# Sums over tokens of a tile in two halves instead of one operation, with the instruction order searched anew

## Chip, cores, metric

One core of one Trainium2 chip. The metric is device time in microseconds (us) of one execution. The kernel before takes 383.95 us (median of 3 runs, 383.66 to 384.04). "Span" is the time from the first to the last instruction in the trace of one execution; it is some 1.8 us shorter than the measured time.

## The reference

Two layers, each of a linear attention (A) and a gated MLP (B), on x of 2048 tokens x 512, with 32 heads of 16 columns and 1376 columns in the MLP. What the change touches are `kv` and `z`, the sums over all tokens:

```python
phi_k = concat([softmax(pk), softmax(-pk)], -1)      # per head; pk = k @ w_phi
kv  = einsum("bhsf,bhsd->bhfd", phi_k, v)            # sum over tokens s
z   = einsum("bhsf->bhf", phi_k)
num = einsum("bhqf,bhfd->bhqd", phi_q, kv)           # attention needs the complete sums
den = einsum("bhqf,bhf->bhq", phi_q, z)[..., None] + 1e-6
x = x + ((num / den) merged) @ wo
...
gate = gate * (gate > 0);  x = x + (gate * up) @ W_down
```

## The kernel before

It works on 16 tiles of 128 tokens. The program describes some 2100 operations with their dependences, buffers and a due time each (table `DUE`) and, for those that two engines can do, a place (`PLACE`: copies out of PSUM on ScalarE or VectorE, halves of phi on GpSimd or VectorE). A planner turns this into one order for every engine; both tables come from a search. TensorE's order therefore isn't in the code but in the tables.

The keys of one tile (cut):

```python
k  = op("PE", ..., name="K")                 # 4 products: pk, with w_phi folded into the weight
e  = [op("ACT", ..., Exp, scale=+1/-1)]      # ek, two halves
v  = op("PE", ..., name="V"); v = evac(...)  # vext: v and a column of ones
a  = op("DVE", SUM16, tensor_reduce(ek))     # sk: sums per head; then Ln and Exp on ScalarE: 1/sum
...
parts = []
for k, e in enumerate(PHI[phi_eng]):         # two halves of 32 rows of heads each
    parts.append(op(e, cost, due, f, [a], ..., name="phi", alt=...))  # phiK = ek * sk, VectorE or GpSimd
a = parts

def kvz():
    for g in range(NG):                      # NG = 8
        b, k = g // 2, g % 2
        nc.tensor.matmul(self.bufs[k].t[:, b * GV:(b + 1) * GV],
                         lhsT=ph.t[:, g, :, :].rearrange("p s e -> p (s e)"), rhs=vx.t[:, g, 0:GV],
                         start=(self.n == 0 and b == 0), stop=(self.n == T - 1), skip_group_check=True)
    self.n += 1
first = not self.sums
z = op("PE", SUMS, due_z, kvz, a + [v] + (self.before if first else self.sums[:1]),
       self.bufs if first else [], [ph, vx] + ([] if first else self.bufs), name="kvz")
self.sums.append(z)
```

After 16 tiles VectorE turns the two PSUM buffers of sums into `R`, and the attention products (`erq`, Eq times R) can start. TensorE then works on projections, gate, up and down products; layer 1's keys lie among them.

Filler products: up to the first sum over tokens, the program puts products on zeros where the plan foresees an idle TensorE:

```python
for o in order:
    if o.eng == "PE":
        filling = filling and o.name != "kvz"
        if filling and free is not None:
            idle(max(0, int((o.start - free - 150) / FILL)))     # products of zeros, 216 ns each
        free = o.start + o.spent
    o.emit()
```

The softmax here doesn't subtract the row's maximum and nothing guards it: scores larger than these inputs give would overflow.

## Time and profile before

| | before |
|---|---|
| time, median | 383.95 us |
| span | 382.0 us |
| TensorE busy, work by count | 371.5 us, 368.8 us |
| VectorE, ScalarE, GpSimd busy | 311.1, 215.0, 41.9 us |
| halves of phi | 38 on GpSimd, 26 on VectorE |

The prediction shows how TensorE bounds the kernel. Two more rows of the kernel before belong to the argument: the makers of phi, in the groups by form (count, then busy us and mean ns of one, then idle time before them).

```profile
L879 POOL TENSOR_TENSOR phiK<-ek,sk 128x512 bf16<-128x512 bf16 x38 | 41.2, 1102 | 192.3 <-ACT sk L870 164.1 <-DVE hT L1076 15.8 <-PE b L849 3.9
L879 DVE TENSOR_TENSOR phiK<-ek,sk 128x512 bf16<-128x512 bf16 x26 | 17.6, 703 | 0.1
```

A half of phi costs VectorE 0.70 us and GpSimd 1.10 us on average. And the view of the tile phiK lists who waited for it (us, times):

```profile
  DVE R L924: 2.0, 2
  POOL phiK L879: 1.9, 1
```

TensorE is not in the list: no sum over tokens was late for its phi.

### The profile page before, as it was taken

To read this page: it belongs to the slowest core of one execution; us is meant where nothing else is said; L and a number is where in the kernel's file an instruction comes from. 1 tells how busy PE (TensorE), PEld (TensorE's weight loads), DVE (VectorE), ACT (ScalarE), POOL (GpSimd) and SP (SyncE) were. 2 spreads that over 40 slices of the span, in tenths; PEclk is the share of its full clock that TensorE was granted. 3 is DMA by queue.
4 is the path that set the end of the run, shared out by engine and by line. 5 is a ranking of instruction groups with operands and counts; after the bars stand their busy time and mean duration, and the time that the engine had idled before them with its cause. 6 is when DMAs were issued, how large, how long until landed. Compare 5 with 4: busy or idle time off the path is not lost.

```text
span 382.0 us, 7622 instructions
## 1 busy us (share of the span) xinstructions
PE 371.5 (97%) x2787; PEld 224.4 (59%) x2832; DVE 311.1 (81%) x798; ACT 215.0 (56%) x554; POOL 41.9 (11%) x44
## 2 busy tenths in 40 slices
PE   7999998999989999999999999999999999999996
PEld 4545456967545445554656654696855544467575
DVE  7999999999999989983694677999998976763334
ACT  6999989636445316772455679984526412243040
POOL 0276710000200000230020124000000000000000
PEclk9999999999999999999999999999999999999999
DMA  8497720222221321211200100013322221020110
GB/s 232 122 205 219 188 89 2 52 58 62 57 56 41 44 54 40 45 23 27 45 6 15 22 8 1 2 36 70 77 44 70 57 56 56 14 62 16 41 50 29
DMA packets 60869, 22.83 MB, mean 60 GB/s; under 512 B 52672, under 2 KB 59808, under 8 KB 60832
## 3 DMA queue, kind: packets, MB, share of 16 engines
q1 hardware_dynamic: 60416, 21.95, 24.9%
q8 instruction: 22, 0.36, 0.4%
q10 hardware_dynamic: 416, 0.39, 0.4%
q14 instruction: 15, 0.12, 0.1%
HBM read 7.91 MB, written 2.10 MB: 26 GB/s over the span
## 4 chain that ended last, share of the span: by engine, by line
PE 77%; DVE 17%; DMA 2%; issue 2%; ACT 1%; DVEq 0%
PE b L1068 31%; PE b L1101 17%; PE b L855 5%; PE b L849 5%; PE b L992 5%; PE b L937 5%; PE q L955 3%; PE b L1044 2%; PE q L896 2%; DMA xnTA<-xn 2%; DVE pr L980 1%; DVE bstA L810 1%; DVE bstB L810 1%; DVE sk L860 1%; DVE N L753 1%
## 5 line engine op out<-in xcount | busy, mean ns | idle before, releaser
L1068 PE MATMUL b<-xnTB,wgu 128*128 128x128 bf16 (+2 forms) x1191 | 152.3, 279 | 0.5
L1068 PEld LDWEIGHTS <-wgu 128*128 128x128 bf16 x1200 | 97.7, 98 | 42.5
L1072 ACT ACTIVATE gu<-b 128x512 bf16<-128x512 f32 (+1 forms) x83 | 48.0, 584 | 63.7 <-PE b L1068 61.3
L1101 PE MATMUL b<-wd,hT 128*128 128x512 bf16 (+3 forms) x349 | 82.3, 372 | 0.7
L879 POOL TENSOR_TENSOR phiK<-ek,sk 128x512 bf16<-128x512 bf16 x38 | 41.2, 1102 | 192.3 <-ACT sk L870 164.1
L1101 PEld LDWEIGHTS <-hT 128*128 128x128 bf16 (+1 forms) x363 | 34.7, 98 | 33.9 <-DVE hT L1076 0.2
L1076 DVE TENSOR_TENSOR hT<-gu 128x512 bf16<-128x512 bf16 (+1 forms) x83 | 34.0, 414 | 15.4 <-ACT gu L752 14.2
L1108 DVE SCALAR_TENSOR_TENSOR X<-b,rsB,X 128x512 bf16<-128x512 f32 (+1 forms) x33 | 23.7, 729 | 23.8 <-PE b L1101 23.8
L752 ACT CAST gu<-b 128x512 bf16<-128x512 f32 (+1 forms) x50 | 28.4, 570 | 24.0 <-PE b L1068 20.4
L860 DVE TENSOR_REDUCE sk<-ek 128x64 f32<-128x1024 bf16 x32 | 38.6, 1210 | 2.7 <-ACT ek L852 2.3
L852 ACT ACTIVATE ek<-b 128x512 bf16<-128x512 f32 x64 | 36.0, 616 | 8.3 <-PE b L849 8.1
L941 ACT ACTIVATE Eq<-b 128x512 bf16<-128x512 f32 x64 | 37.3, 629 | 3.3 <-PE b L937 3.1
L752 ACT CAST N<-q 128x384 bf16<-128x384 f32 (+1 forms) x59 | 26.1, 464 | 12.4 <-PE q L955 6.7
L855 PE MATMUL b<-wv,xnTA 128*128 128x512 bf16 x123 | 31.9, 379 | 0.3
L937 PE MATMUL b<-xnTA,Wq 128*128 128x512 bf16 x125 | 31.9, 379 | 0.2
L849 PE MATMUL b<-Wk,xnTA 128*128 128x512 bf16 x123 | 31.6, 379 | 0.4 <-DVE xnTA L753 0.2
L992 PE MATMUL b<-wo,oT 128*128 128x512 bf16 x120 | 31.3, 379 | 0.4
L753 DVE CAST gu<-b 128x512 bf16<-128x512 f32 (+1 forms) x33 | 21.8, 665 | 11.1 <-PE b L1068 11.1
L955 PE MATMUL q<-R,Eq 128*128 128x144 bf16 x256 | 27.5, 226 | 1.8 <-DVE N L753 1.3
L955 PEld LDWEIGHTS <-Eq 128*128 128x128 bf16 x256 | 20.3, 98 | 13.1 <-issue 2.6
L980 DVE TENSOR_TENSOR pr<-N,w 128x1024 bf16<-128x1024 bf16 x32 | 21.8, 683 | 0.7
L810 DVE BATCH_NORM_STATS2 bstA<-X 128x6 f32<-128x512 bf16 x32 | 21.3, 682 | 1.2 <-DMA X<-in_A_x_dram 1.0
(75 smaller groups left out, 388.9 us busy)
## 6 DMA issues: line engine op xcount, KB each, us to landing
out_dram<-X SPq DMA_DIRECT2D x15, 128.0 KB, 1.7
X<-in_A_x_dram SPq DMA_DIRECT2D x6, 256.0 KB, 3.3
wgu<-in_B_W_gate_dram SPq DMA_DIRECT2D x4, 344.0 KB, 3.4
wgu<-in_B_W_up_dram SPq DMA_DIRECT2D x4, 344.0 KB, 3.5
wd<-in_B_W_down_dram SPq DMA_DIRECT2D x5, 256.0 KB, 3.5
wv<-in_A_wqkv_dram SPq DMA_DIRECT2D x2, 256.0 KB, 4.7
wo<-in_A_wo_dram SPq DMA_DIRECT2D x4, 128.0 KB, 3.1
oT<-o SPq DMA_TRANSPOSE x28, 2.3
```

Of the source, the lines that this page charges most:

```text
L752: both = {"ACT": ("ACT", act(cols), lambda: nc.scalar.copy(out=out_(), in_=in_()), False), "DVE": ("DVE", dve(cols), lambda: nc.vector.ten ...
L849: k = op("PE", mm(4, 512), due, lambda: [nc.tensor.matmul(kp.t[:], lhsT=xnTA[c][:, b, cols], rhs=Wk2[:, b, :], start=(b == 0), stop=(b == ...
L855: v = op("PE", mm(4, 512), due_v, lambda: [nc.tensor.matmul(vp.t[:], lhsT=xnTA[c][:, b, cols], rhs=wv[:, b, :], start=(b == 0), stop=(b == ...
L860: a = op("DVE", SUM16, due, lambda: nc.vector.tensor_reduce(out=sk.t[:, row, :], in_=ek.t[:].rearrange("p g s (h f) -> p (g s h) f", f=DH) ...
L879: e.tensor_tensor(out=ph.t[:].rearrange("p g s (h f) -> p (g s h) f", f=DH)[:, lo:lo + n], in0=ek.t[:].rearrange("p g s (h f) -> p (g s h) ...
L937: q = op("PE", mm(4, 512), due(c, b), lambda b=b, qp=qp: [nc.tensor.matmul(qp.t[:], lhsT=Wq2[:, m, b * P:(b + 1) * P], rhs=xnTA[c][:, m, : ...
L941: done.append(op("ACT", act(512), due(c, b), lambda b=b, s=s, qp=qp: nc.scalar.activation(out=Eq[c][:, b, s, :], in_=qp.t[:], func=AF.Exp, ...
L955: pe.append(op("PE", mm(len(groups), GE), due, lambda ps=ps, groups=groups: [nc.tensor.matmul(ps.t[:, n * GE:(n + 1) * GE], lhsT=Eq[c][:, ...
L992: a = op("PE", mm(4, 512), due + 3, lambda: [nc.tensor.matmul(yp.t[:], lhsT=oT.t[:, b, :], rhs=wo[:, b, :], start=(b == 0), stop=(b == NB ...
L1068: nc.tensor.matmul(ps.t[:, q * W:(q + 1) * W], lhsT=wgu[:, s, b, g * P:(g + 1) * P], rhs=xT.t[:, b, 0:W], start=(b == 0), stop=(b == NB - 1))
L1072: nc.scalar.activation(out=gu.t[:, 0, 0:cols], in_=gp.t[:, 0:cols], func=AF.Relu)
L1101: nc.tensor.matmul(yp.t[:, 0:c1 - c0], lhsT=h.t[:m, f * W + i * P:f * W + (i + 1) * P], rhs=wd[:m, f, c0:c1], start=(f == 0), stop=(f == N ...
```

## The change

The intent: the first four products of a tile need only the first half of phi, so let them go as their own operation once that half is there, and search the order anew with this freedom. The diff, cut to its core:

```diff
-            self.n = 0
+            self.n = [0, 0]
...
-            def kvz():
-                for g in range(NG):
+            def kvz(lo, hi):
+                for g in range(lo, hi):
...
-                                     start=(self.n == 0 and b == 0), stop=(self.n == T - 1),
+                                     start=(self.n[0] == 0 and b == 0), stop=(self.n[lo // 4] == T - 1),
...
-            z = op("PE", SUMS, due_z, kvz, a + [v] + (self.before if first else self.sums[:1]),
-                   self.bufs if first else [], [ph, vx] + ([] if first else self.bufs), name="kvz")
-            self.sums.append(z)
+            for n in range(2):
+                z = op("PE", (SUMS[0] / 2, SUMS[0] / 2 + 170), due_z + n, lambda n=n: kvz(4 * n, 4 * n + 4), [a[n], v] + (
+                    self.before if first and not n else self.sums[:1]), self.bufs if first and not n else [],
+                    [ph, vx] + ([] if first and not n else self.bufs), name="kvz")
+                self.sums.append(z)
```

and all of PLACE and DUE (2105 entries become 2137) replaced. In the new order the two halves of a tile stand 0 to 18 TensorE operations apart, and in 10 of the 32 tiles (16 in each layer) the second half goes first. Lines moved: phi L879 is L681 after, the sums L896 are L698, attention products L955 are L760, key products L849 are L651, values L855 are L657, R L918 and L924 are L723 and L729, copies on ScalarE and VectorE L752 and L753 are L554 and L555. (The tile names say what is what.)

## The prediction

> **What bounds the kernel now.** I read the page's busy shares, then TensorE's waits, then the chain that ended last, and at last TensorE's own sequence from start to end, counting what its matmuls need.
>
> ```profile
> PE 371.5 (97%) x2787; PEld 224.4 (59%) x2832; DVE 311.1 (81%) x798; ACT 215.0 (56%) x554; POOL 41.9 (11%) x44
> ...
> PE 77%; DVE 17%; DMA 2%; issue 2%; ACT 1%; DVEq 0%
> ```
>
> TensorE is busy 97% of 382.0 us and carries 77% of the chain that ended last. Busy time of a pipelined engine may hide gaps, so I also took the rate. Two lines of the chain in order of time and one of the groups by form:
>
> ```profile
> 28.46 0.86 PE b L849 x4
> ...
> 129.71 2.59 PE b L1068 x12
> ...
> L896 PE MATMUL q<-vext,phiK 128*128 128x65 bf16 x256 | 12.9, 193 | 0.1
> ```
>
> Four matmuls of 512 columns take 0.86 us, 216 ns each: 512/2.4 + 2.5 ns. The third line is the operation that the change touches (vext and phi summed over tokens): 256 matmuls, which had TensorE idle for 0.1 us in all before them. So no sum over tokens has ever held TensorE up for want of its phi.
>
> With columns/2.4 + 2.5 ns for each of the 2832 matmuls that the program issues (counted in its instruction order, as some matmul records are missing from the trace), the work is 368.8 us: 1186 of 512 columns x 0.2158 = 256.0; 422 of 256 x 0.1092 = 46.1; 584 of 128 x 0.0558 = 32.6; 256 of 144 x 0.0625 = 16.0; 128 of 192 x 0.0825 = 10.6; 256 of 65 x 0.0296 = 7.6. Subtracting that running sum from the start times in the timeline gives where the other 13.2 us go:
> - 2.6 before 4.4 us: 1.2 until the first matmul, 1.4 for matmuls at half rate.
> - 2.8 from there to the first attention product at 54.4 us (1.9 of it before 18 us, while x and weights arrive and are normalised and turned).
> - 2.3 between 54.6 and 65 us, where the sums have just been turned into R and the first tiles' attention has nothing beside it.
> - 1.2 at 104.6 to 107.1 us, one wait.
> - 1.2 in all the rest of the 310 us.
> - 3.1 after the last matmul: the last residual sums and the store.
>
> The waits of TensorE agree (line waited for, us, times, longest):
>
> ```profile
> PE q L955 <- DVE N L753: 1.3, 2, 1.1
> ...
> PE b L797 <- DVE o L985: 1.0, 2, 0.6
> ...
> PE q L955 <- DVE R L924: 0.3, 1, 0.3
> ```
>
> L955 is the attention product, which needs a PSUM buffer that VectorE still has to empty; L797 turns o. The only place where the sums over tokens stand near a wait is the end of layer 0's keys (timeline, VectorE and TensorE):
>
> ```profile
> 49.07 3.09 DVE L879 TENSOR_TENSOR phiK<-ek,sk 128x512 bf16<-128x512 bf16 x5
> 52.52 0.37 DVE L924 SCALAR_TENSOR_TENSOR R<-q,Mf 64x16 bf16<-64x16 f32 x2 [0.36 <-PE q L896]
> ...
> 51.56 0.95 PE L896 MATMUL q<-vext,phiK 128*128 128x65 bf16 x24
> ...
> 54.40 0.35 PE L955 MATMUL q<-R,Eq 128*128 128x144 bf16 x3 [0.16 <-DVE R L918]
> ```
>
> The last phi ends at 52.16, VectorE waits 0.36 us for the last tile's products, and TensorE works on query products meanwhile and waits 0.16 us.
>
> **What the Trainium skill says.** "TensorE: Matmul & The Clock Gate", section "Back-to-back issue gap", gives N/2.4 + 2.5 ns warm; the trace agrees (216 ns at 512). The same section gives about 131 ns as a sustained spacing at N=512; this trace doesn't show that, so I use 216. "Perfetto Trace Analysis", "Identifying the Most-Contended Engine", warns that matmul busy time is no measure of the distance to the limit, hence the count above. "PSUM — Partial Sum Buffer", "The four PSUM rules": the flag of a group's first matmul clears a whole bank, later groups in it must not set it. The change keeps it on the first half of the first tile alone, so it stays correct; no duration here shows it. "GPSIMD Engine Reference", "Specifications": GpSimd shares its SBUF interfaces with VectorE. The trace agrees: while GpSimd made phi (102.53 to 103.59), a VectorE add that takes 205 ns on average took 0.98:
>
> ```profile
> 102.53 1.06 POOL L879 TENSOR_TENSOR phiK<-ek,sk 128x512 bf16<-128x512 bf16 x1 [0.41 <-ACT sk L870]
> 102.66 0.98 DVE L973 TENSOR_TENSOR m<-m 128x32 f32<-128x32 f32 x1
> ```
>
> That add is in the chain to the 1.1 us wait listed above.
>
> **The change part by part.**
> 1. The sums: 32 operations of 8 products become 64 of 4. Still 256 products of 65 columns, 7.6 us. No work goes, and no matmul is added. A first half may start one phi half earlier: 0.70 us (VectorE, mean of that row) or 1.10 us (GpSimd). As TensorE waited 0.1 us for these, the direct gain is at most that, plus what comes at the two ends of the keys: after the last phi half 4 products instead of 8 are left, 0.13 instead of 0.26 us, twice. Some 0.2 us in all. The buffers of phi and vext come free no sooner, since the second half holds them.
> 2. The tables of order and placement are replaced, so every engine's order differs: this is the larger part. From the instruction orders: VectorE loses 17 evictions of N (8 x 546 + 9 x 402 ns = 8.0 us) and 17 of DS (8 x 196 + 9 x 177 = 3.2) and gains 8 of gu (8 x 681 = 5.4): 5.7 us less. ScalarE gets the opposite, 8 x 498 + 9 x 384 + 8 x 224 + 9 x 198 - 8 x 586 = 6.3 us more, at 56% busy. GpSimd keeps 38 halves of phi. VectorE's relief falls where it is nearly full (19.5 of 20 us from 60 to 80, 19.9 from 80 to 100, 19.2 from 100 to 120), but TensorE loses only 2.3 + 1.2 us there.
> 3. Filler matmuls on zeros, put where the tables foresee an idle TensorE before the first sum: 18 instead of 13, 5 x 0.216 = 1.1 us more work. They mostly fill idle time (0.9 us of it is seen at 4.4 to 8.0), but the first key product now comes after 9.2 us of work instead of 5.5, and VectorE and ScalarE are full from 10 to 50 us (9.5 to 10.0 of each 10), so what is started late there is not made up. The first attention product comes after 50.1 us of work instead of 49.0.
> 4. Distances in TensorE's order, in us of work: from the end of a tile's attention products to its projection, the first two tiles 3.1 and 2.8 (before 3.0 and 2.6), in layer 1 4.6 and 4.2 (4.6 and 5.2); from the last key product to the last sum 6.8 and 7.2 (before 5.9 and 6.1). So the critical ends get about as much cover as before. The tail is alike: the last gate and up products end 2.2 us of work before the end instead of 3.1, the chain behind them (eviction 0.4, product 0.29, with latencies some 1.0) is still covered, and then comes the same half-width sum and store, 3.1 us.
>
> Sum: work 369.9; start 2.6; up to the first attention product 2.1 (2.8, less what the fillers take up, plus the later keys); transition 2.1; the wait near 105 us 0.6 (half: less VectorE work, but GpSimd still interferes); all the rest 1.2; tail 3.1. That makes 381.6 us against 382.0 now. The measured time is 383.95 for a span of 382.0, 1.95 more, so 383.5; I say 383.4.
>
> **The rivals.** *A gain of several us* because the sums no longer wait for both halves: for it speak the size of the rewrite and VectorE's 81%. Against it, L896's idle 0.1 us, and the floor: with every wait gone after the start, the work of 369.9 plus 2.6 and 3.1 is 375.6 of span, 377.5 measured, which is only 1.7% below 383.95. Two per cent (376.3) is out of reach unless the fillers go too. A good new order would give 380 to 382. *A loss*: an order that was searched less well makes new waits; ScalarE gets more evictions where it also does Exp, and an attention product then waits for ScalarE as it did for VectorE. Three or four waits of the size at 105 us would give 387 to 388; nothing in the distances of step 4 shows one, but GpSimd's interference moves and can't be counted from the order. *The start*: if the later keys are not absorbed, the whole 1.1 us of fillers and some of the 3.7 us of delay come through, 385 to 386.
>
> **Range and chances.** The gain is bounded by 6.4 us and likely a tenth of that; a loss is open upwards but needs several new waits. Hence 381.2 to 386.8, faster by over 2% 0.02, within 0.94, slower by over 2% 0.04.
>
> **What would show it.** Idle time before the sums still near 0.1 us; TensorE's work clock at 1.1 us more at the first attention product; VectorE's busy time down by some 5 us and ScalarE's up by 6, with the time hardly moved; the wait near 105 us smaller or elsewhere; the tail at 3.1 us. I am wrong if the span moves more than 3 us: then look for waits of attention products on evictions (slower), or for a transition under 1 us and a start under 2 us (faster).

## The result, and the profile after

| | before | after |
|---|---|---|
| time, median (range, runs) | 383.81 (383.61 to 384.04, 4) | 386.76 (385.88 to 387.13, 4) |
| span of the profiled run | 382.0 | 385.3 |
| TensorE's work by count | 368.8 | 369.9 |

The ratio is 1.0073, with a 95% interval of 1.0055 to 1.0092: slower by 0.7%. Ratios here and below are the mean time of one kernel's fast runs over that of the other's of the same rounds, so not quite the ratio of the medians quoted. The profiled run of after was its slowest (387.13), which will matter.

The busy line of the page after, and its chain's shares:

```profile
PE 376.3 (98%) x2837; PEld 224.6 (58%) x2837; DVE 310.2 (80%) x772; ACT 218.7 (57%) x580; POOL 42.6 (11%) x44
...
PE 88%; DVE 6%; ACT 3%; issue 1%; DMA 1%; POOL 0%; DVEq 0%; ACTq 0%; POOLq 0%
```

The busy shares look better than before (TensorE 98%, the chain 88% on TensorE), and the kernel is slower. ScalarE has 3.7 us more, VectorE only 0.9 us less, though it does 26 instructions fewer.

TensorE's waits after (us, times, longest):

```profile
PE b L599 <- DVE o L790: 0.8, 2, 0.5
...
PE q L698 <- DVE phiK L681: 0.7, 1, 0.7
...
PE q L760 <- DVE R L729: 0.4, 1, 0.4
PE q L760 <- DVE R L723: 0.4, 1, 0.4
...
PE q L698 <- POOL phiK L681: 0.2, 1, 0.2
```

The 1.1 us wait of an attention product for the copy of N is gone, and there is what was never there before: sums that wait for phi. Phi's makers after, and who waited for it:

```profile
L681 POOL TENSOR_TENSOR phiK<-ek,sk 128x512 bf16<-128x512 bf16 x38 | 41.9, 1126 | 194.7 <-ACT sk L672 180.4 <-PE b L657 7.5 <-DVE X L913 6.9
L681 DVE TENSOR_TENSOR phiK<-ek,sk 128x512 bf16<-128x512 bf16 x26 | 22.0, 868 | 0.2 <-ACT sk L672 0.2
```

```profile
  PEld L698: 4.1, 9
  PE q L698: 0.9, 2
...
```

The same 26 halves on VectorE take 868 ns instead of 703: 4.4 us more, out of the 5.7 us of VectorE time that the prediction counted as saved.

**Where the 3.3 us of span went.** I take the same clock as in the prediction: the lag is the start time of a product minus the work of all products issued before it (columns/2.4 + 2.5 ns each). A lag that grows is time in which TensorE fell behind its own rate.

| at | lag before | lag after | added since the row above |
|---|---|---|---|
| first attention product (54.40, 57.33 us) | 5.39 | 7.23 | +1.84, of it 1.04 by 18 us of work |
| 60 us of work (transition) | 7.67 | 9.38 | -0.13 |
| 150 us of work (before has its wait near 105 us) | 9.03 | 9.59 | -1.15 |
| 220 us of work (after has its 0.7 us wait for phi) | 9.22 | 10.63 | +0.85 |
| 260 us of work (turn to layer 1's attention) | 9.89 | 12.12 | +0.82 |
| end of the work | 10.15 | 12.17 | -0.21 |
| tail | 3.08 | 3.26 | +0.18 |
| five more filler products, 0.216 each | | | +1.08 |

The last column sums to 3.3. Of the 2.9 us that the first attention product comes later, 2.1 (1.04 of lag and the five fillers) are there by 18 us of work, at 22.6 us into the span in before and 23.7 in after. The end of layer 0's keys in the timeline after, to be held against the prediction's:

```profile
52.00 2.73 DVE L681 TENSOR_TENSOR phiK<-ek,sk 128x512 bf16<-128x512 bf16 x4
...
55.25 0.86 DVE L723 TENSOR_TENSOR R<-q,Mf 64x256 bf16<-64x256 f32 x2 [0.52 <-PE q L698]
...
57.33 0.35 PE L760 MATMUL q<-R,Eq 128*128 128x144 bf16 x3 [0.39 <-DVE R L729]
```

All of it is some 2.9 us later than before, and VectorE's wait for the last sums before it makes R is no shorter (0.52 us against 0.36): having halves has not let them come sooner.

### The profile page after: what moved, and what is told of

It is laid out like the page before. It is cut to its first block, busy times and chain, and to the rows that moved or that the text cites. A ratio compares the mean times of both kernels' runs of the same rounds, so it can differ in the third digit from the quotient of the medians.

```text
span 385.3 us, 7680 instructions
## 1 busy us (share of the span) xinstructions
PE 376.3 (98%) x2837; PEld 224.6 (58%) x2837; DVE 310.2 (80%) x772; ACT 218.7 (57%) x580; POOL 42.6 (11%) x44
## 4 chain that ended last, share of the span: by engine, by line
PE 88%; DVE 6%; ACT 3%; issue 1%; DMA 1%; POOL 0%; DVEq 0%; ACTq 0%; POOLq 0%
PE b L873 36%; PE b L906 19%; PE b L797 7%; PE b L651 7%; PE b L657 6%; PE b L742 5%; PE q L760 4%; PE b L849 3%; PE q L698 2%; DVE bstA L612 1%; DVE sk L662 1%; DMA X<-in_A_x_dram 1%; DVE R L723 1%; ACT N L554 1%; PE b L599 1%
## 5 line engine op out<-in xcount | busy, mean ns | idle before, releaser
L873 PE MATMUL b<-xnTB,wgu 128*128 128x128 bf16 (+2 forms) x1200 | 150.5, 279 | 0.0
L906 PE MATMUL b<-wd,hT 128*128 128x512 bf16 (+2 forms) x363 | 82.8, 373 | 0.0
L681 POOL TENSOR_TENSOR phiK<-ek,sk 128x512 bf16<-128x512 bf16 x38 | 41.9, 1126 | 194.7 <-ACT sk L672 180.4
L654 ACT ACTIVATE ek<-b 128x512 bf16<-128x512 f32 x64 | 35.2, 610 | 14.6 <-PE b L651 13.7
L554 ACT CAST N<-q 128x384 bf16<-128x384 f32 (+1 forms) x76 | 33.2, 456 | 12.7 <-PE q L760 9.6
L746 ACT ACTIVATE Eq<-b 128x512 bf16<-128x512 f32 x64 | 36.0, 628 | 5.7 <-PE b L742 5.5
L555 DVE CAST gu<-b 128x512 bf16<-128x512 f32 (+1 forms) x41 | 27.3, 672 | 10.0 <-PE b L873 9.9
L797 PE MATMUL b<-wo,oT 128*128 128x512 bf16 x128 | 32.7, 379 | 0.0
L657 PE MATMUL b<-wv,xnTA 128*128 128x512 bf16 x128 | 32.2, 379 | 0.4 <-ACT xnTA L554 0.4
L651 PE MATMUL b<-Wk,xnTA 128*128 128x512 bf16 x128 | 31.7, 379 | 0.0
L554 ACT CAST gu<-b 128x512 bf16<-128x512 f32 (+1 forms) x42 | 23.8, 568 | 12.5 <-PE b L873 11.9
L760 PE MATMUL q<-R,Eq 128*128 128x144 bf16 x256 | 27.8, 226 | 1.4 <-ACT DS L554 0.4
L760 PEld LDWEIGHTS <-Eq 128*128 128x128 bf16 x256 | 20.4, 98 | 12.6 <-issue 2.3
```

What stands on the lines that cost most here:

```text
L554: both = {"ACT": ("ACT", act(cols), lambda: nc.scalar.copy(out=out_(), in_=in_()), False), "DVE": ("DVE", dve(cols), lambda: nc.vector.ten ...
L651: k = op("PE", mm(4, 512), due, lambda: [nc.tensor.matmul(kp.t[:], lhsT=xnTA[c][:, b, cols], rhs=Wk2[:, b, :], start=(b == 0), stop=(b == ...
L657: v = op("PE", mm(4, 512), due_v, lambda: [nc.tensor.matmul(vp.t[:], lhsT=xnTA[c][:, b, cols], rhs=wv[:, b, :], start=(b == 0), stop=(b == ...
L681: e.tensor_tensor(out=ph.t[:].rearrange("p g s (h f) -> p (g s h) f", f=DH)[:, lo:lo + n], in0=ek.t[:].rearrange("p g s (h f) -> p (g s h) ...
L746: done.append(op("ACT", act(512), due(c, b), lambda b=b, s=s, qp=qp: nc.scalar.activation(out=Eq[c][:, b, s, :], in_=qp.t[:], func=AF.Exp, ...
L760: pe.append(op("PE", mm(len(groups), GE), due, lambda ps=ps, groups=groups: [nc.tensor.matmul(ps.t[:, n * GE:(n + 1) * GE], lhsT=Eq[c][:, ...
```

## Experiments

The candidates at the start:
- Theory 1: the split does nothing; the new order costs, and mainly that of layer 0's keys.
- Rival a: the split itself costs (more waits on semaphores, halves in separate places).
- Rival b: the fillers cost their 1.1 us.
- Rival c: the late first key product costs, as the prediction's third rival says.
- Rival d: the waits for phi in layer 1 cost.

Before the first run I compared compiled programs. The order of before, with the split written in and the two halves left side by side, gives the same instructions with the same waits as before, without one line of difference: in 26 of the 32 tiles the weight load of the fifth product already had its own wait on the second half of phi (in the other six it has none in either program). So in the old kernel the first four products could already go ahead as soon as the first half was there. The split alone changes nothing; only a different order can.

In the experiments each engine's order is written out as a list of operation numbers, taken from one kernel or the other, in place of due times. All ran correctly. "Before" in each is the kernel before in the same rounds.

### Is it the split? (e1, e2)

e1: the order of before, with the split, and in 29 of 32 tiles the first half moved up by 1 to 41 TensorE operations, to where its phi should be there.

```diff
 SEQ["PE"] of before:
-  ..., other operations, sum(tile, half 0), sum(tile, half 1), ...
+  ..., sum(tile, half 0), other operations, sum(tile, half 1), ...
```

> The order and placement of the kernel before, with each first half of a tile's sums moved up in TensorE's sequence to where its half of phi should be ready, by 1 to 41 operations for 29 of the 32 tiles. Theory 1 (the split itself is worth nothing, because the sums never waited): 383.8 us, within 0.6 of the kernel before. Theory 2 (64 pieces instead of 32 cost TensorE waits or switching): 385 or more. If the split has a gain of its own: under 383.2.

Measured: 385.01 us against 384.18, ratio 1.0022 (1.0010 to 1.0035). The split used as it was meant, in an order that is otherwise old, gives nothing and costs 0.8 us. By its number that is what was expected under Theory 2 (385 or more), not Theory 1; but the compiled programs and e2 say that it is not the pieces that cost, so it must be where they stand. The weight loads of the sums, which waited for no phi in before, now wait for VectorE's four times (1.5 us in all): the first halves stand where their phi is only just made, and what would have filled that time comes later. That the 0.8 us come from these waits is likely, but not shown.

e2: the order of after, with each tile's two halves joined at the place of the later one.

```diff
 SEQ["PE"] of after:
-  ..., sum(tile, half 0), other operations, sum(tile, half 1), ...
+  ..., other operations, sum(tile, half 0), sum(tile, half 1), ...
```

> The order and placement of the changed kernel, with the two halves of each tile's sums put together again where the later of them stood. Theory 1 (the loss comes from the new order of everything else): 386.7 us, within 0.7 of the changed kernel; perhaps 0.7 less where the wait at 188 us for VectorE's phi (0.7 us) goes with the half that was moved. Theory 2 (the split costs): back towards 384.

Measured: 386.55 against 384.18, ratio 1.0068 (1.0054 to 1.0082); after had 1.0073. With the split undone, all of the loss stays. Rival a falls, and so does any story in which the split did something: everything is in the order and the placement.

### Which part of the order? (e3, e4)

e3 takes every engine's order up to layer 0's first attention product from before and the rest from after (the same operations but for five of the query products and their Exp); e4 the other way round.

```diff
-  SEQ[engine] = after
+  SEQ[engine] = before[: first attention product] + after[that :]      # e3
+  SEQ[engine] = after[: first attention product] + before[that :]      # e4
```

> Everything up to layer 0's first attention product in the order and placement of the kernel before, all the rest as in the changed kernel. Theory 1 (the keys of layer 0 cost 2.9 of the 3.3 us): 384.2 us, about 2.6 below the changed kernel; 13 fillers instead of 18. Theory 3 (the new placement of evictions on ScalarE and the new order of the rest cost): 386 or more.

> The reverse: everything up to layer 0's first attention product as in the changed kernel, all the rest in the order and placement of the kernel before. Theory 1: 386.6 us, 2.8 above the kernel before. Theory 3: under 385.

Measured: e3 385.14 (ratio 1.0023, 1.0010 to 1.0035), so the rest of the order costs 1.0 us against before; e4 386.46 (1.0060, 1.0048 to 1.0073), so layer 0's keys cost 2.3. Theory 1 met its number in e4 (386.6) and missed it by 0.9 in e3 (384.2): the rest costs something too. Together 3.3, against 2.95 measured for the whole. Two thirds and more are in the first 57 us. The rest is a balance: the removed wait near 105 us gives 1.1 back, layer 1 takes 1.7 (by the table of the lag).

### The fillers (e5)

```diff
-                    idle(max(0, int((o.start - free - 150) / FILL)))
+                    0                # only the eight products ahead of everything stay
```

> The changed kernel without the ten filler matmuls that it puts between real work in the first 13 us (the eight at the very start stay). Theory 1 (the fillers only fill idle time that is there anyway, because the first key product is ordered late): within 0.4 us of the changed kernel, 386.7. Rival (fillers are work on TensorE's path): 385.7, 1.1 less for the five extra ones, or 384.6, 2.2 less for all ten.

Measured: 388.21 against 383.97, ratio 1.0111 (1.0093 to 1.0128): slower than after by some 1.5 us, with ten products fewer. Neither theory had that. The windows of two stretches show why, first of e5, then of after (length, busy TensorE, weight loads, VectorE, ScalarE, GpSimd; granted clock; DMA share, GB/s):

```profile
8.00:12.00 4.00, 1.55 (x19) 1.04 (x17) 4.00 (x13) 2.74 (x9) 0.00 (x0) 0.91 0.75 170
12.00:16.00 4.00, 3.35 (x24) 2.02 (x24) 3.51 (x9) 2.18 (x8) 0.00 (x0) 0.66 0.59 171
```

```profile
8.00:12.00 4.00, 3.44 (x26) 1.63 (x25) 4.00 (x12) 2.66 (x9) 0.00 (x0) 1.00 0.83 173
12.00:16.00 4.00, 3.62 (x31) 2.08 (x30) 4.00 (x12) 2.80 (x10) 0.00 (x0) 1.00 0.49 119
```

With TensorE busy 1.55 of 4 us, the granted clock fell to 0.66 in the next 4 us, just when real products came. (In the trace it is 0.50 from 11.32 to 14.73 us.) The Trainium skill says as much in "TensorE: Matmul & The Clock Gate", section "What's actually happening": the clock depends on how busy the engine has been. All five runs of e5 have a mean clock under 1 (0.996 four times, 0.991 in the slowest, 389.39 us), those of after 0.999 to 1.000. (The share of 4 us alone doesn't decide it: in e6 a stretch with 1.42 of 4 us busy was followed by 1.00.) So here fillers are not a cost that can simply be counted in the sum: without them the clock is lost. That the ten as a whole cost time is refuted; whether the five extra ones cost something of their own was not tested, as e5 took out all ten. So rival b stays open in that smaller form.

### The late first key product (e6, e9)

After has its first key product at 14.77 us, before at 9.63, since the last quarter of the key weight is copied late, by VectorE at 14.05. In the timelines (before's window ended at 10 us, hence two products):

```profile
9.63 0.59 PE L849 MATMUL b<-Wk,xnTA 128*128 128x512 bf16 x2
...
14.77 3.61 PE L651 MATMUL b<-Wk,xnTA 128*128 128x512 bf16 x16
```

e6: the first 129 operations (to the first sum) in before's order, the rest in after's.

```diff
-  SEQ[engine] = after
+  SEQ[engine] = before[: first sum over tokens] + after[that :]
```

> Only the start, up to the first sum over tokens (129 operations on all engines), in the order and placement of the kernel before; everything after it as in the changed kernel, the end of layer 0's keys included. If the late first key product (14.8 us instead of 9.6) is what costs: 384.6 us, some 2.1 below the changed kernel. If it is absorbed and the end of the keys costs by itself: 386 or more.

Measured: 389.33 against 383.97, ratio 1.0136 (1.0119 to 1.0153), 2.6 us worse than after. TensorE's waits in e6:

```profile
PE q L663 <- DVE phiK L646: 4.3, 3, 2.6
...
PE q L663 <- POOL phiK L646: 1.0, 1, 1.0
```

The start is faster: the product that starts when 14 us of real work are done (fillers after the first eight not counted) is 5.74 us later than that work alone would have it, as in before (5.63), where after is 7.74 us late. But the sums then wait for phi, 5.3 us in all, 4.7 of it in the first 60 us. Before that GpSimd had idled 4.07 us for the `sk` of its halves, and one VectorE half took 0.84 us more beside GpSimd. As this could be the seam between two orders, e9 moves as little as possible: in after's start four operations (the expectation says five; the edit has four), namely the copy of the last quarter of the key weight to ScalarE and ahead, the first key product, and two of its Exp.

```diff
 SEQ:
-  DVE: ..., copy(key weight, quarter 4), ...        # starts 14.05
+  ACT: ..., copy(v, tile 0), copy(key weight, quarter 4), ..., Exp(tile 0) x2 earlier
-  PE:  ..., fold, fold, ..., K(tile 0), ...         # starts 14.77
+  PE:  ..., fold, K(tile 0), fold, ...
```

> The changed kernel with five operations moved in its start and nothing else: the eviction of the fourth quarter of the folded key weight from VectorE, where it stands behind 22 others and starts at 14.05 us, to ScalarE right behind the first eviction of V (some 9 us); the first key product up behind the next fold, and its two Exps up on ScalarE. If the late key weight is what costs the start: the first key product near 10 us instead of 14.8, and a gain between 0.9 us (only that product's time in idle TensorE) and 2.3 us: 384.5 to 385.9. If something else sets the start: 386.7.

Measured: 390.14 against 384.02, ratio 1.0166 (1.0152 to 1.0180), the worst of all but one. The first key product did come at 9.40 us. What happened later, in the timeline of e9 (start, length):

```profile
24.86 3.57 POOL L646 TENSOR_TENSOR phiK<-ek,sk 128x512 bf16<-128x512 bf16 x3 [0.97 <-ACT sk L637]
...
25.99 1.54 DVE L646 TENSOR_TENSOR phiK<-ek,sk 128x512 bf16<-128x512 bf16 x1
...
27.58 0.30 PE L663 MATMUL q<-vext,phiK 128*128 128x65 bf16 x4 [2.00 <-DVE phiK L646]
```

VectorE's half of phi took 1.54 us, TensorE waited 2.0 us for it, and after a stretch with TensorE busy for 1.95 of 4 us the granted clock of the next 4 us (28 to 32) was 0.58 (from the windows of e9). The clock is not what makes e9 slow: two of its five runs kept a mean clock of 1.000 and took 389.88 and 390.14 us, the three at 0.996 took 390.08 to 391.12. So an earlier first key product alone saves nothing: with 14 us of real work done, e9 is 7.53 us late, and the kernels with after's keys 7.21 to 7.74, as the product that needs the next data waits until 13.45 for ScalarE's copy of the turned x, and the other key products come at 14.99. In this narrow form rival c falls. In the wider form, that the order of the whole start costs, it does not: e6 had 1.5 to 2.0 us of it back by 19.9 us, and lost them and more where the two orders meet. The next reading comes back to this.

### The waits in layer 1, and two runs that did not work out (e10, e7, e8)

e10: after, with the half sum that waited 0.7 us at 189 us moved behind the next two operations (four products).

```diff
 SEQ["PE"] of after, layer 1:
-  ..., 1026, 1222, 1160, 1025, ...      # 1026: half sum
+  ..., 1222, 1160, 1026, 1025, ...
```

> The changed kernel with one half sum of layer 1 (four products) put two operations later on TensorE, behind the gate or up product and the key product that followed it, so that its half of phi, which VectorE made in 1.50 us instead of 0.70 while GpSimd made another, is ready. If that wait is real time: 0.8 us less, 385.9. If the wait is only moved on: 386.7.

Measured: 386.17 against 384.02, ratio 1.0063 (1.0049 to 1.0076), against 1.0073 of after: inside the noise. TensorE's wait only moved on to the sum that comes next, as e10's list of waits has it:

```profile
PE q L663 <- DVE phiK L646: 0.6, 1, 0.6
```

So rival d cannot be tested by moving one sum; phi itself was late.

e7 was to be the best of both: before's order to the first attention product, after's for the middle, before's from the turn to layer 1's attention on.

```diff
-  SEQ[engine] = before
+  SEQ[engine] = before[: attention, layer 0] + after[: attention, layer 1] + before[that :]
```

> Layer 0's keys as in the kernel before; from its first attention product to layer 1's first attention product as in the changed kernel; the rest as in the kernel before. Adding up what TensorE idled in each third: 383.5 us, 0.3 below the kernel before, and 0.7 below the kernel with only the keys taken back. If thirds disturb each other (what is left over at the seams): 384 to 386.

Measured: 388.24 against 383.97, ratio 1.0111 (1.0096 to 1.0127). Its lag grows from 9.8 to 13.6 us between 230 and 240 us of work, at the second seam, by waits of 0.7 to 0.8 us for DS, o and w. Why these operations are late there was not followed further; the run only says that parts of two orders can't be put together freely.

e8: the new code with before's tables, each half with its whole's due time, planned anew.

```diff
-DUE = (..., d, ...)
+DUE = (..., d, d, ...)          # one entry more for every sum over tokens
```

> The split with the kernel before's tables of due times and placement, each half of a sum given the due time of the whole, nothing searched anew. If the split by itself leaves the plan nearly alone: 383.8 us. If the planner, given 32 more operations, reorders what follows and the old table no longer fits: 386 to 392. The order of instructions says the second: it differs from the kernel before's throughout.

Measured: 408.77 against 383.97, ratio 1.0651 (1.0629 to 1.0672), slower. The planner decides otherwise at many places, and attention products wait for copies out of PSUM all through the kernel. The longest entry in its list of TensorE's waits (us, times, longest):

```profile
PE q L963 <- ACT DS L757: 4.3, 8, 0.7
```

It says nothing of the split. It says that the tables fit one set of operations, and that after's tables had to be searched anew to get back to where before was.

### What in the keys? A reading of all traces

e6 and e9 also point at phi on VectorE beside phi on GpSimd. The prediction quoted the Trainium skill on a shared interface. The page "SBUF — State Buffer", section "Who interferes with whom", is more exact: VectorE instructions with two inputs in SBUF contend with a GpSimd instruction that reads SBUF. Of VectorE's two-port modes, another case than phi's two inputs, it says "Whoever issues first gets the shared pair for the whole instruction; the other **fully blocks** (not throttle)." The traces show nearly that for phi too, instruction by instruction. Ten of VectorE's halves of phi in after started inside a half of GpSimd. In us, with the time from the start to the end of the GpSimd half that ran then:

| starts at | GpSimd's half still runs for | VectorE's half took | difference |
|---|---|---|---|
| 35.02 | 0.18 | 0.731 | 0.55 |
| 37.08 | 0.60 | 1.148 | 0.55 |
| 45.54 | 1.01 | 1.556 | 0.55 |
| 52.00 | 0.37 | 0.922 | 0.55 |
| 187.35 | 0.95 | 1.501 | 0.55 |
| 206.05 | 0.32 | 0.871 | 0.55 |
| 206.85 | 1.00 | 1.545 | 0.55 |
| 231.35 | 0.41 | 0.958 | 0.55 |
| 235.98 | 0.42 | 0.967 | 0.55 |
| 236.87 | 0.99 | 1.543 | 0.55 |

A half alone takes 0.68 (median). So a VectorE half that starts inside a GpSimd half takes what is left of that one, plus 0.55. It waits for the other's end, and only some 0.13 of its own time lie in the wait. (Where less than 0.13 is left it loses nothing: before's half at 103.56 had 0.03 left and took 0.68.) The add of 0.18 us alone that took 0.98 in before fits as well (0.93 left at 102.66). Two kinds of VectorE instruction with one SBUF input were not delayed: 35 sums `sk` and 19 statistics that lay beside a GpSimd half in the two traces took at most 0.014 us more than the median of those that did not. (xn, with one tensor and columns of scalars as inputs, took 0.67 and 0.88 us more in 2 of 12.)

Who comes first can hang on hundredths. The same pair in after (VectorE, then GpSimd, both from the timeline; the second of GpSimd's two starts at 45.50):

```profile
44.48 2.07 POOL L681 TENSOR_TENSOR phiK<-ek,sk 128x512 bf16<-128x512 bf16 x2
...
45.54 1.56 DVE L681 TENSOR_TENSOR phiK<-ek,sk 128x512 bf16<-128x512 bf16 x1 [0.23 <-ACT sk L672]
```

and in e10, which has the same order up to there (the second of GpSimd's starts at 44.97):

```profile
43.95 2.56 POOL L646 TENSOR_TENSOR phiK<-ek,sk 128x512 bf16<-128x512 bf16 x2
...
44.91 0.69 DVE L646 TENSOR_TENSOR phiK<-ek,sk 128x512 bf16<-128x512 bf16 x1
```

In after GpSimd was first by 0.04 us, and VectorE took 1.56; in e10 VectorE was first by 0.06, took 0.69, and GpSimd paid.

Now all fourteen traces: what VectorE's instructions lost beside GpSimd's phi in the first 60 us (duration less the median of the same instruction with no GpSimd phi beside it, where that is over 0.1 us), and how late TensorE is (start less the work before it; fillers after the first eight not counted as work) at two places: when 14 us of this real work are done, and at the first attention product.

| kernel | lost beside GpSimd, 0 to 60 us | delay at 14 us of real work | delay of the first attention product |
|---|---|---|---|
| e3 (before's keys) | 0 | 5.67 | 6.37 |
| e7 (before's keys) | 0 | 5.77 | 6.43 |
| before | 0 | 5.63 | 6.46 |
| e11 (before's keys) | 0 | 5.98 | 6.76 |
| e12 (before's keys) | 0 | 5.90 | 6.84 |
| e1 (before's keys, first sums early) | 0 | 5.97 | 7.55 |
| e10 (after's keys) | 0.71 | 7.21 | 8.06 |
| e8 (planned anew) | 0.87 | 5.57 | 8.17 |
| e2 (after's keys, sums joined) | 0.72 | 7.41 | 8.30 |
| e4 (after's keys) | 1.39 | 7.34 | 8.43 |
| after | 1.59 | 7.74 | 9.40 |
| e5 (no fillers) | 1.28 | 8.24 | 9.89 |
| e6 (seam at the first sum) | 3.16 | 5.74 | 11.92 |
| e9 (four operations moved) | 3.47 | 7.53 | 12.19 |

The first and the last column go together (correlation 0.97, slope 1.6). But the middle column says that this is not where most of the keys' loss comes from. It is taken 19.7 to 22.3 us into the span, in every kernel before its first instruction that lost time to GpSimd (in after that one comes at 37.08 us). There the four kernels with after's keys (e2, e4, e10, after) are 7.43 us late on average, the five plain ones with before's keys 5.79: 1.63 of the 1.97 us by which they differ at the first attention product (8.55 against 6.57). From there on they fall behind by another 1.12 and 0.78.

In the keys of before's trace no VectorE half of phi started inside a GpSimd half: they fall in GpSimd's pauses or just ahead of it. In after's, four did.

How far is this shown? The lock and its price per instruction are. What it costs the kernel is a reading: no run took the meetings away and left the rest of the order alone. After's keys lose 1.1 us to it on average (e2, e4, e10, after), but only 0.34 us of the difference between the two orders is left for everything that comes after the first 22 us. Where the lock shows is between runs of after's keys: from the middle column to the last, the three in which GpSimd was first near 45 us (after, e4, e5) fall behind by 1.1 to 1.7 us, the two in which VectorE was first (e2, e10) by 0.8 to 0.9. It also adds to what e6 and e9 lose. The 1.6 us of the start are its own: e6, with before's start, doesn't have them, and e9 says that the late key weight alone is not the reason. Which operations of the start are, stays open, and so does whether the five extra fillers, which stand in this stretch (1.08 us), cost any of it.

In layer 1 (from 180 us on) the same count gives 0.59 us in before and 3.80 in after. There one link can be followed to TensorE, in the timeline of after:

```profile
186.24 2.07 POOL L681 TENSOR_TENSOR phiK<-ek,sk 128x512 bf16<-128x512 bf16 x2 [6.87 <-DVE X L913]
...
187.35 1.50 DVE L681 TENSOR_TENSOR phiK<-ek,sk 128x512 bf16<-128x512 bf16 x1
...
188.91 0.30 PE L698 MATMUL q<-vext,phiK 128*128 128x65 bf16 x4 [0.67 <-DVE phiK L681]
```

VectorE's half is blocked for 0.82 us (1.50 less 0.68), and the sum waits 0.67 us for it. From 60 to 180 us it is the other way: 2.69 us in before, 0.80 in after. Of the 2.69, 1.0 lie at 102 to 104 us, ahead of the wait near 105 us, which the new order does remove.

### Can the wait near 105 us be had without the new order? (e11, e12)

e11: before, with one attention product (two of 2832 matmuls) moved behind gate and down products that are ready.

```diff
 SEQ["PE"] of before:
-  ..., 900, 903, 655, 906, 844, 941, ...      # 655: the attention product that waited 1.1 us
+  ..., 900, 903, 906, 844, 655, 941, ...
```

> The kernel before, with two of its 2832 matmuls moved: the attention product that waited 1.1 us for VectorE at 106 us is put behind the gate product and the three down products that followed it. No split, no new table. If that wait is real time on the path: 1.2 us less, 382.7, faster than both kernels. If it comes back at a later wait: 383.9.

Measured: 383.89 against 384.02, ratio 0.9997 (0.9985 to 1.0010). The wait came back one operation on, for another thing that VectorE was late with; the next product of TensorE in e11's timeline:

```profile
108.05 0.82 PE L871 MATMUL b<-wd,hT 128*128 128x512 bf16 x3 [0.81 <-DVE hT L846]
```

So it is not TensorE's order; VectorE's backlog is the candidate. In before, two VectorE halves of phi of layer 1, needed much later, stand right in it, as before's timeline shows:

```profile
103.56 0.68 DVE L879 TENSOR_TENSOR phiK<-ek,sk 128x512 bf16<-128x512 bf16 x1
...
105.16 0.68 DVE L879 TENSOR_TENSOR phiK<-ek,sk 128x512 bf16<-128x512 bf16 x1
...
107.14 0.22 PE L955 MATMUL q<-R,Eq 128*128 128x144 bf16 x1 [1.06 <-DVE N L753]
```

e12: these two moved to an idle stretch of VectorE at 135 us, and nothing else.

```diff
 SEQ["DVE"] of before:
-  792, 898, 576, 605, 748, 606, 1045, 899, 607, 796, 608, ..., 950, 972, ...
+  792, 898, 576, 605, 606, 1045, 899, 607, 608, ..., 950, 748, 796, 972, ...
```

> The kernel before, with two VectorE instructions moved and nothing else: the two halves of phi of layer 1's first two tiles that VectorE makes at 103.6 and 105.2 us, in its fullest stretch, are put just ahead of where it idles 1.4 us at 135 us; their sums come at 145 us. If VectorE's lateness (1.4 us of phi in front of the eviction that the attention product waits for) is the wait at 106 us: TensorE's 1.2 us there go and the time is 382.8, faster than both kernels. If GpSimd's interference or the next link of the chain sets it: 383.5 to 384.

Measured: 383.39 (382.95 to 383.75) against 383.94 (383.70 to 384.79), ratio 0.9984 (0.9970 to 0.9997). It beats both kernels, by 0.55 us over before, about half of what the wait was worth; the interval barely excludes no gain at all, and the gain is far below 2%. The same attention product in e12's timeline:

```profile
106.57 0.28 PE L725 MATMUL q<-R,Eq 128*128 128x144 bf16 x2
```

The attention product starts 0.57 us earlier, and the timeline puts no idle time ahead of it. The lag grows by 0.28 us from 90 to 100 us of work, where before's grows by 1.23: in this stretch 0.95 us are gained, and the profiled run of e12 had started 0.39 us later (8.07 us of lag at 90 us of work against 7.68). So VectorE's backlog was the wait. (The add that GpSimd's phi lengthens to 0.98 us is still there; what went is the work that stood behind it.)

## Why the prediction was right or wrong

The range (381.2 to 386.8) held 386.76, by 0.04 us, and one of the four runs (387.13) lies outside it: that is luck. "Within 2%" was given 0.94 and came. The direction was missed: 383.4 predicted, half a us less than before, and it became 2.95 more. Its own sign of being wrong, a span that moves by more than 3 us, came in the profiled run (3.3); it said to look for waits on evictions, and they were elsewhere. (One slip in the sum: the 1.95 us from span to time pairs the span of a run of 383.81 us with the median of 383.95; in one and the same run it is 1.8.) By the terms of the sum, in us of span:

| term | predicted | measured |
|---|---|---|
| work | 369.9 | 369.9 |
| start | 2.6 | 2.7 |
| up to the first attention product | 2.1 | 4.5 |
| transition | 2.1 | 2.15 |
| wait near 105 us | 0.6 | 0.0 |
| all the rest | 1.2 | 2.8 |
| tail | 3.1 | 3.3 |
| sum | 381.6 | 385.3 |

- Step 1 (the split: some 0.2 us of gain at most): right, and stronger than put. It is nothing at all (e1, e2, and the compiled programs are alike). The sign I had in hand was the 0.1 us of idle time. The other, that the fifth weight load already waits by itself, could have been looked up before predicting.
- Step 2 (copies move from VectorE to ScalarE, 5.7 us less and 6.3 more): ScalarE got 3.7 more, VectorE lost only 0.9. The count of copies was right in kind; what was missed is phi, whose 26 VectorE halves took 4.4 us more in the same number. Step 2 took every instruction at its mean of before, though the prediction had shown an add that took five times as long beside GpSimd's phi.
- Step 3 is the one that failed: "They mostly fill idle time", with 2.1 us left up to the first attention product, 0.7 less than before. It took 4.5 in the profiled run, 1.7 more than before. Of that 0.9 arose by 18 us of work, ahead of any meeting of VectorE's phi with GpSimd's, and 0.8 later; in e10, which has the same order of keys but lost 0.88 us less beside GpSimd, the later part is 0.8 us smaller. So the prediction's third rival had the place right, a start that isn't absorbed, and nearly the size (385 to 386). Its two parts can't simply be taken out: without fillers the clock is lost (e5), and the key weight early alone gains nothing clear at the start (e9). What step 3 did not have at all is the later part: as far as the traces tell, VectorE's phi falling inside GpSimd's.
- Step 4 (the critical ends keep their cover): right for layer 0's transition and the tail; in layer 1 the turn to attention took 0.8 us more than before, and the stretch with the wait at 189 us another 0.85. That is the term "all the rest", 1.6 too small. The second rival ("new waits", on copies by ScalarE) was right that there would be new waits, and wrong on which: the one followed up in layer 1 was for phi.
- The wait near 105 us was put at half and went away wholly. From 100 to 110 us GpSimd makes no phi any more (busy 2.1 of 10 us in before) and VectorE one half (at 103.42) instead of two. Which of the two counted more isn't separated for after; in e12 moving VectorE's two halves was enough.
- "GpSimd's interference moves and can't be counted from the order", said of the second rival, is where the range should have been made lopsided upwards: the risk was named, and then only gains and small losses were summed.

One more caution on the 4.5: the profiled run of after was its slowest of four. Three profiles of kernels with after's keys ran 387.13 (after, VectorE second at 45.5 us), 385.97 (e10, VectorE first) and 385.46 (e2, VectorE first too). That suggests that part of the scatter of this family, 385.5 to 387.3, wider than before's, comes from such tosses; three profiles don't prove it.

What stays open: what in the order of the start costs the 1.6 us that are there by 22 us; what the five extra fillers cost; e7's seam; and whether an order with after's middle and no meetings in the keys would beat e12.

## What to carry to other kernels

Before splitting an operation so that it can start earlier, look whether its instructions already wait part by part: here the fifth weight load did in 26 of 32 tiles, and the split could bring nothing. When a change comes with a newly searched order, compare the same order with and without the change, and the parts of the orders against each other: the order was all of the difference. Before a loss is put down to an effect that goes with it, look when it arises: here 1.6 of the keys' 2.0 us were there before VectorE and GpSimd first met. Where these two both work from SBUF, read the durations of single instructions and not their mean. And two instructions moved out of VectorE's fullest stretch (e12, 0.55 us gained) did more than a rewritten order of 2100 operations.

## What the Trainium skill lacked or had wrong

- "TensorE: Matmul & The Clock Gate", section "Back-to-back issue gap": its sustained spacing of about 131 ns at N=512 is in none of these traces. 216 ns held throughout; with columns/2.4 + 2.5 ns the lag of before moves by 0.03 us from 260 to 340 us of work. Nor does its 81 ns at N=128 bind here: sixteen products of 128 columns, each with its weight load, took 1.06 us in e7, 66 ns each with the last one's latency counted in.
- "GPSIMD Engine Reference", section "Specifications", names the shared interface but no size. "SBUF — State Buffer", section "Who interferes with whom", has the rule for two inputs in SBUF, and the traces agree with it; it gives no duration for this pair, and says "fully blocks" of the two-port modes alone. For phi it is not quite that. A blocked half took what was left of the GpSimd instruction, plus the instruction's own time less 0.13 us (ten of ten halves of phi in after, within 0.01), so up to 0.88 us on a half of 0.68. That the order of issue decides it does say, but not that 0.04 to 0.06 us may settle it, so that two programs with the same order up to there (after, e10) differ.
- "TensorE: Matmul & The Clock Gate", section "What's actually happening", speaks of an idle window. Here a stretch of 4 us with TensorE busy for 1.55 (e5) or 1.95 us (e9) was followed by a mean granted clock of 0.66 or 0.58 in the next 4. The section gives no measure of how thin a stream of products still holds the clock, and these runs give none either: in after 3.44 of 4 us did, but so did 1.42 of 4 us in e6 (24 to 28 us, followed by 1.00).
